# Chunked attention and a token-mixing layer: one transposed token weight for both batches, attention in four array tiles, a fixed skewed order

## The chip, the cores and the metric

The kernel runs on one core of one Trainium2 chip. The time is device microseconds (us) of one execution. An execution that was profiled has its own time, and beside it the span, from the first to the last instruction of the profile.

The engines are PE (TensorE, matrix products, with its weight loads as PEld), DVE (VectorE), ACT (ScalarE, functions by table), POOL (GpSimd) and SP (SyncE). Here POOL gives out the loads from memory and SP the stores and two transfers inside the on-chip memory. Each engine runs its own instructions in a fixed order and waits at semaphores for the others.

## The reference

Eight batches, 8 heads, 576 tokens, 64 values a head. Tokens are cut into chunks of 64, and attention stays inside a chunk. Its result x (576 x 512 a batch) goes through a layer that mixes tokens by two 576 x 576 weights and channels by a 512 x 512 one:

```python
# q, k, v: (8, 8, 576, 64) -> chunks (8, 8, 9, 64, 64)
scores = scale * np.matmul(q_c, k_c.transpose(0, 1, 2, 4, 3))
scores = scores - np.max(scores, axis=-1, keepdims=True)
attn = np.exp(scores)
attn = attn / (np.sum(attn, axis=-1, keepdims=True) + 1e-09)
out = np.matmul(attn, v_c)
x = np.ascontiguousarray(attn_out.transpose(0, 2, 1, 3)).reshape(B, S, H * D)

theta = x @ w_theta
cos_t, sin_t = (np.cos(theta), np.sin(theta))
zr = x * cos_t
zi = x * sin_t
yr = np.einsum('ts,bsd->btd', w_tok_r, zr)
yi = np.einsum('ts,bsd->btd', w_tok_i, zi)
y = yr + yi
u = x + y
return (u + np.maximum(u @ w_ch, 0.0)).astype(np.float32)
```

Inputs and output are float32; the kernel works in float16 with float32 sums and turns the inputs to float16 while it loads them.

## The kernel before

Batches are taken in four pairs. A pair has 1152 tokens, nine tiles of 128. Tiles 0 to 3 belong to the first batch, 5 to 8 to the second, and tile 4, the mid tile, holds the last 64 tokens of the first and the first 64 of the second. The tiles are worked on in five groups (0 1), (2 3), (4), (5 6), (7 8).

The steps of a group:

- `load_qk` and `load_v` (L103 to L117): one POOL transfer for each of q, k and v of a tile, two for the mid tile; q and k go into a pool of 6 buffers (`nat`), v into 18 slots, half of them for each pair in turn.
- `a1` (L167): PE transposes q and k of a group (tile `ps_qkT`, 16 transpositions for two tiles), DVE copies the result out.
- `a2` (L187): the score matmuls, 64 x 64 each. Heads lie in pairs on the two halves of the rows, and the two chunks of a tile go to the two halves of the output partitions, so that four array tiles are in use. ACT takes exp.
- `a3` (L212): attention times v, with a column of ones for the sum. Both the input rows and the output partitions of a matmul are those of its chunk, so that two array tiles are in use. DVE takes the reciprocal of the sum and multiplies: x.
- `a4` (L238): PE transposes x, ACT copies it to xT.
- `a5` (L254): theta on PE (`ps_theta`), ACT makes cos and sin, DVE makes zr and zi. The mid tile is special: each batch needs the cos and the sin product of its 64 tokens, stacked on 128 partitions, so one half product of each is moved to the other half of the partitions through a tile `zmid` by two SP transfers (L296, L297).
- `y` (L299): for one batch and a block of 128 channels, 18 matmuls of 288 columns contract over the 128-row blocks of zr, of zi and of the stacked mid tile with the transposed token weight `wT`. DVE adds xT and writes uT.
- `w` (L327): for one tile, the channel product and u itself (by the identity) on PE, relu on ACT, the sum o on DVE, and a store.

`tok_w` (L133) makes a block of the transposed token weight. Since the second batch's tokens begin in the middle of a tile, its blocks are cut 64 rows later than the first batch's; there are two transposed weights, `wT[0]` and `wT[1]`, each of nine blocks.

All results of PE go through four PSUM buffers of one kind (`psum2`), taken in turn by whichever step comes next; a step's first matmul waits until the result four steps back has been read out.

The order is set in two ways. `weave` (L16) puts the filler steps evenly between the main steps, by their number, and a scheduler in the framework then moves instructions among the engines' queues by its own priorities, so that the program's order on PE is near to the written one but not the same. For pair 0 the written order is: attention of the first batch beside the first token weight; the first batch's y beside the second batch's attention and the second token weight; the second batch's y beside the scores of pair 1; the outputs beside the attention of pair 1. For later pairs it is: the first batch's y beside the whole next pair's scores, then y and w in turn beside the whole next pair's attention.

The softmax here doesn't subtract the row's maximum and nothing guards it: scores larger than these inputs give would overflow.

## Time and profile before

| | us |
|---|---|
| three runs | 245.6, 246.23, 246.33 |
| median | 246.23 |
| profiled execution | 245.5 |
| its span | 243.4 |
| PE busy | 208.7 (86%) |
| DVE busy | 129.1 (53%) |
| ACT busy | 111.2 (46%) |
| POOL busy (it gives out loads) | 105.9 (44%) |
| mean granted PE clock | 0.979 |

The stages of the span, cut at the y matmuls, are 0 to 39.4 (loads, and attention of the first batch of pair 0), 39.4 to 71.2 (its y, and the second batch's attention), 71.2 to 113.1 (second y and outputs of pair 0), 113.1 to 162.4 (pair 1), 162.4 to 211.7 (pair 2) and 211.7 to 243.4 (pair 3, which has nothing beside it).

In the profile a matmul's duration holds the time until its result is through the array, so the sum of durations is more than PE's time; the distance from one start to the next in the chain of waits is what a group of matmuls costs. A "releaser" is what ended an engine's wait. In lines of the timeline, the first column is the start and the second the length.

### The profile page before, as it was taken

What the parts mean: (1) busy time and instruction counts of PE and PEld (TensorE: products, weight loads), DVE (VectorE), ACT (ScalarE), POOL (GpSimd) and SP (SyncE); (2) the same over time, 40 slices, a digit from 0 to 9 for tenths busy, and PEclk for the clock granted to TensorE, in tenths of its full rate; (3) what the DMA queues carried; (4) which work ended last, traced back from release to release, by engine and by line L of the source; (5) the groups of instructions that cost most, each with busy time, mean ns of one, the idle gap of its engine ahead of it and who ended that gap; (6) DMA issues with size and microseconds to landing.
All of it is one profiled execution on the core that took longest, in us unless ns stands there. A gap on an engine that the chain in (4) does not pass through costs nothing.

```text
span 243.4 us, 6143 instructions
## 1 busy us (share of the span) xinstructions
PE 208.7 (86%) x2692; PEld 143.6 (59%) x2692; DVE 129.1 (53%) x217; ACT 111.2 (46%) x136; POOL 105.9 (44%) x133
## 2 busy tenths in 40 slices
PE   0453799289999979899998998999989989999992
PEld 0232566156578856456876764658867645577761
DVE  0223327424457466686754637868447377653353
ACT  2012289134862257688414283884132738810132
POOL 9997497869928997220998000008000000000000
PEclk9999999758999999999999999999999999999999
DMA  7999999999999999993999511439901213400226
GB/s 47 145 135 168 185 155 176 166 140 103 148 87 59 149 146 186 211 143 110 81 149 143 89 66 43 131 109 66 69 3 47 86 41 94 148 3 0 89 88 215
DMA packets 120698, 26.89 MB, mean 110 GB/s; under 512 B 113376, under 2 KB 116064, under 8 KB 120672
## 3 DMA queue, kind: packets, MB, share of 16 engines
q0 software_dynamic: 114784, 16.54, 99.1%
q1 hardware_dynamic: 5888, 9.96, 11.8%
q8 instruction: 21, 0.34, 0.6%
q14 instruction: 5, 0.04, 0.0%
HBM read 33.06 MB, written 9.44 MB: 175 GB/s over the span
## 4 chain that ended last, share of the span: by engine, by line
PE 71%; DVE 8%; POOL 7%; DMA 6%; ACT 5%; issue 1%; POOLq 0%; DVEq 0%
PE ps_y L312 30%; PE ps_uw L332 11%; PE ps_theta L261 11%; PE ps_qkT L176 5%; POOL qk L108 4%; DMA wnat<-in_moe_w_tok_r_dram 4%; PE ps_x L223 3%; PE ps_xT L245 3%; PE ps_wT L144 3%; PE ps_uw L339 3%; DMA zr<-zmid 2%; POOL v L116 2%; PE ps_sT L198 2%; DVE x L231 2%; ACT cos L271 2%; DVE qkT L183 2%
## 5 line engine op out<-in xcount | busy, mean ns | idle before, releaser
L108 POOL DMA_DIRECT2D qk<-in_q_dram x40 | 35.8, 904 | 54.2 <-PE ps_qkT L176 49.0
L320 DVE TENSOR_TENSOR uT<-ps_y,xT 128x576 f16<-128x576 f32 x32 | 24.2, 757 | 46.7 <-PE ps_y L312 46.7
L312 PE MATMUL ps_y<-wT,zr 128*128 128x288 f16 x288 | 44.4, 293 | 4.2 <-DMA zr<-zmid 4.0
L332 PE MATMUL ps_uw<-wch,uT 128*128 128x512 f16 x144 | 42.6, 380 | 3.2 <-DVE x L231 2.3
L345 ACT ACTIVATE relu<-ps_uw 128x512 f32<-128x512 f32 x36 | 21.5, 598 | 46.4 <-PE ps_uw L339 46.2
L205 ACT ACTIVATE eT<-ps_sT 128x1024 f16<-128x1024 f32 (+1 forms) x20 | 18.4, 938 | 50.7 <-PE ps_sT L198 50.7
L312 PE MATMUL ps_y<-wT,zi 128*128 128x288 f16 x288 | 41.5, 290 | 0.0
L116 POOL DMA_DIRECT2D v<-in_v_dram x40 | 34.3, 895 | 7.6 <-PE ps_x L223 7.1
L108 POOL DMA_DIRECT2D qk<-in_k_dram x40 | 35.8, 909 | 2.4 <-DMA wnat<-in_moe_w_tok_r_dram 1.8
L312 PEld LDWEIGHTS <-zr 128*128 128x128 f16 x288 | 26.9, 99 | 12.9 <-DMA zr<-zmid 4.2
L261 PE MATMUL ps_theta<-wtheta,xT 128*128 128x512 f16 x144 | 33.7, 379 | 0.5 <-DVE o L347 0.5
L312 PEld LDWEIGHTS <-zi 128*128 128x128 f16 x288 | 28.6, 99 | 7.7
L176 PE MATMUL ps_qkT<-id,qk 128*128 128x128 f16 x288 | 22.1, 231 | 11.5 <-DMA qk<-in_q_dram 9.7
L339 PE MATMUL ps_uw<-id,uT 128*128 128x128 f16 x144 | 31.5, 219 | 0.0
L183 DVE COPY qkT<-ps_qkT 128x2048 f16<-128x2048 f16 (+1 forms) x20 | 22.0, 1114 | 17.1 <-PE ps_qkT L176 16.1
L347 DVE TENSOR_TENSOR o<-ps_uw,relu 128x512 f32<-128x512 f32 x36 | 24.7, 688 | 10.7 <-ACT relu L345 10.5
L176 PEld LDWEIGHTS <-qk 128*128 128x128 f16 x288 | 18.1, 102 | 14.0 <-DMA qk<-in_q_dram 10.6
L332 PEld LDWEIGHTS <-uT 128*128 128x128 f16 x144 | 14.0, 97 | 17.9 <-DVE x L231 3.5
L231 DVE TENSOR_TENSOR x<-ps_x,recip 128x512 f16<-128x512 f32 x36 | 24.2, 688 | 0.7
L271 ACT ACTIVATE cos<-ps_theta,pihalf 128x1024 f16<-128x1024 f32 (+1 forms) x20 | 20.7, 1034 | 7.7 <-PE ps_theta L261 7.5
L250 ACT COPY xT<-ps_xT 128x1024 f16<-128x1024 f16 (+1 forms) x20 | 18.6, 928 | 12.3 <-PE ps_xT L245 12.3
L261 PEld LDWEIGHTS <-xT 128*128 128x128 f16 x144 | 13.4, 98 | 14.9 <-issue 0.8
(35 smaller groups left out, 181.0 us busy)
## 6 DMA issues: line engine op xcount, KB each, us to landing
out_dram<-o SPq DMA_DIRECT2D x32, 256.0 KB, 2.1
qk<-in_q_dram POOLq DMA_DIRECT2D x32, 128.0 KB, 5.2
qk<-in_k_dram POOLq DMA_DIRECT2D x32, 128.0 KB, 5.6
v<-in_v_dram POOLq DMA_DIRECT2D x32, 128.0 KB, 4.9
out_dram<-o SPq DMA_DIRECT2D x8, 128.0 KB, 3.1
wnat<-in_moe_w_tok_r_dram POOLq DMA_DIRECT2D x1, 576.0 KB, 9.1
wnat<-in_moe_w_tok_i_dram POOLq DMA_DIRECT2D x1, 576.0 KB, 11.0
qk<-in_q_dram POOLq DMA_DIRECT2D x8, 64.0 KB, 5.3
```

The source lines that it names most:

```text
L108: nc.gpsimd.dma_start(t[pp : pp + n, ti], ap[2 * p + bb, :, s0 : s0 + n, :].rearrange("h s d -> s h d"),)
L116: nc.gpsimd.dma_start(v16[pp : pp + n, slot, :, 0:D], v[2 * p + bb, :, s0 : s0 + n, :].rearrange("h s d -> s h d"),)
L176: nc.tensor.transpose(psv[:, w, e, jj * P : jj * P + P], t[:, w, 2 * e : 2 * e + 2, :].rearrange("s h d -> s (h d)"), id16,)
L183: nc.vector.tensor_copy(out=qkT[:, :, :, 0 : n * P], in_=psv[:, :, :, 0 : n * P])
L231: nc.vector.tensor_tensor(out=st[p]["x"][:, j, :].rearrange("s (f h d) -> s f h d", f=2, h=NE), in0=px[:, :, :, 0:D], in1=recip.broadcast_ ...
L261: nc.tensor.matmul(ps[:, jj * DM : jj * DM + DM], st[p]["xT"][:, db, j * P : j * P + P], wtheta16[:, db, :], start=(db == 0), stop=(db == ...
L271: nc.scalar.activation(out=cos[:, 0:n].rearrange("p a e -> p (a e)"), in_=pin, func=AF.Sin, bias=pihalf, scale=1.0,)
L312: nc.tensor.matmul(psv[:, hf, 0:HS], z[:, j, db * P : db * P + P], wT[bb][:, kt, hf * HS : hf * HS + HS], start=(i == 0), stop=(i == 2 * KT),)
L320: nc.vector.tensor_tensor(out=s["uT"][:, db, sl].rearrange("p (f c) -> p f c", f=2), in0=psv[:, :, 0:HS], in1=s["xT"][:, db, sl].rearrange ...
L332: nc.tensor.matmul(ps[:, 0:DM], uT[:, db, j * P : j * P + P], wch16[:, db, :], start=(db == 0), stop=(db == NDB - 1),)
L339: nc.tensor.matmul(ps[:, DM + db * P : DM + db * P + P], uT[:, db, j * P : j * P + P], id16,)
L347: nc.vector.tensor_tensor(out=o, in0=ps[:, DM : 2 * DM], in1=r, op=ALU.add)
```

## The change

**The token weight.** The tiles of the second batch are no longer cut at 128 of the pair's tokens, but at 128 of its own: tiles 5 to 8 hold its tokens 0 to 511, and the mid tile the last 64 tokens of both batches (`in_ranges`). Both batches now use the same blocks of one transposed weight `wT`, and `tok_w` runs nine times, not eighteen. The output tiles (`out_ranges`) stay as they were. xT is kept in batch order, so the mid tile's columns are first copied to `xTm` by ACT and then by POOL into the two places in xT. z is kept in tiles for each batch (`z`, `zm`). The natural weight lies in two tiles.

**Attention.** The v chunks of a group of two tiles are loaded so that, for each chunk, rows and output partitions of the attention matmuls can differ: three transfers (64, 128, 64 rows) in place of two. The scores of a chunk are put on matching partitions (`c0 = (n * kh + i) * CH`). The matmuls of two tiles then use four combinations of row half and output half, and a step of `a3` covers half of the heads of two tiles. The mid tile runs as before.

**The order.** The scheduler is switched off (`manual_schedule`), so that each engine runs its instructions in the written order. `weave` spreads the filler by written costs. The mid tile is taken second in its batch's groups, `B0 = [0, 2, 1]`, and `B1 = [3, 4]`. The batches are skewed: beside the first batch's y now stands the attention of the second batch of the same pair; beside the second batch's y and four of the w stand the scores of the whole next pair; beside the other five w stands the attention of the first batch of the next pair. The `nat` pool has 14 buffers. The ones of v and the constant are set by DVE, and the identity is made after the first seven loads. The half products of the mid tile that have to be moved are made first.

```diff
 def weave(main, filler):
-    n, m = len(main), len(filler)
-    done = 0
-    for i, step in enumerate(main):
+    total = sum(c for c, _ in main)
+    rest = sum(c for c, _ in filler)
+    gone, spent = 0.0, 0.0
+    queue = list(filler)
+    for cost, step in main:
         step()
-        want = ((i + 1) * m) // n
-        while done < want:
-            filler[done]()
-            done += 1
+        gone += cost
+        while queue and (spent + queue[0][0] / 2) * total <= gone * rest:
+            cf, f = queue.pop(0)
+            f()
+            spent += cf
+    for _, f in queue:
+        f()
...
+    NAT = 14
-    nat = ctx.enter_context(tc.tile_pool(name="nat", bufs=6))
+    nat = ctx.enter_context(tc.tile_pool(name="nat", bufs=NAT))
+    ctx.enter_context(tc.manual_schedule())
-    wT = [glob.tile([P, 2 * KT + 1, S], FP16, name=f"wT{i}") for i in range(2)]
-    wnat = glob.tile([P, KT + 1, 2, S], FP16, name="wnat")
+    wT = glob.tile([P, 2 * KT + 1, S], FP16, name="wT")
+    wnat = [pairp.tile([P, KT + 1, S], FP16, name=f"wnat{i}", bufs=1)
+            for i in range(2)]
-    nc.gpsimd.memset(v16[:, :, :, D : D + 1], 1.0)
+    nc.vector.memset(v16[:, :, :, D : D + 1], 1.0)
+    nc.vector.memset(pihalf, math.pi / 2.0)
...
+    def in_ranges(j):
+        if j < MID:
+            return [(0, 0, j * P, P)]
+        if j > MID:
+            return [(0, 1, (j - MID - 1) * P, P)]
+        return [(0, 0, KT * P, CH), (CH, 1, KT * P, CH)]
...
+    def x_col(j):
+        return j * P if j < MID else S + (j - MID - 1) * P
...
-    def load_v(p, j):
-        slot = (p % 2) * NT + j
-        for pp, bb, s0, n in tok_ranges(j):
+    def load_v(p, g):
+        j0, n = GROUPS[g]
+        slot = (p % 2) * NT + j0
+        if n == 1:
+            parts = [(slot,) + r for r in in_ranges(j0)]
+        else:
+            _, bb, s0, _ = in_ranges(j0)[0]
+            parts = [
+                (slot, 0, bb, s0, CH),
+                (slot + 1, 0, bb, s0 + CH, P),
+                (slot, CH, bb, s0 + 3 * CH, CH),
+            ]
+        for sl, pp, bb, s0, m in parts:
             nc.gpsimd.dma_start(
...
-    def tok_w(par, kt):
+    def tok_w(kt):
...
+            z=[[pairp.tile([P, KT, DM], FP16, name=f"z{ri}{bb}", bufs=1)
+                for ri in range(2)] for bb in range(2)],
+            zm=[pairp.tile([P, DM], FP16, name=f"zm{bb}", bufs=2)
+                for bb in range(2)],
...
     def a2(p, g):
...
+        for i in range(n):
             for e in range(NE):
                 for par in range(2):
-                    for cp in range(2):
-                        sl = slice(jj * P + cp * CH, jj * P + cp * CH + CH)
+                    for kh in range(2):
+                        c0 = (n * kh + i) * CH
...
-    def a3(p, j, g):
+    def a3(p, g, hg):
...
+        for hh in range(NE if n == 2 else H):
+            h = hg * NE + hh
+            f0, h4 = hh // NE, hh % NE
+            cols = slice(h4 * (D + 1), (h4 + 1) * (D + 1))
+            for i in range(n):
+                for kh in range(2):
+                    half = i if n == 2 else kh
+                    nc.tensor.matmul(
+                        psv[half * CH : half * CH + CH, kh if n == 2 else f0, cols],
+                        eT[kh * CH : kh * CH + CH, i, h // 2, h % 2, :],
+                        v16[kh * CH : kh * CH + CH, slot + (i ^ (kh if n == 2 else 0)), h, 0 : D + 1],
+                    )
...
     def a4(p, g):
...
+        xT = st[p]["xT"]
+        if n == 2:
+            nc.scalar.copy(out=xT[:, :, x_col(j0) : x_col(j0) + n * P], in_=psv)
+            return
+        xm = trig.tile([P, NDB, P], FP16, name="xTm", bufs=1)
+        st[p]["xTm"] = xm
+        nc.scalar.copy(out=xm, in_=psv)
+        for bb in range(2):
+            nc.gpsimd.tensor_copy(
+                out=xT[:, :, bb * S + KT * P : (bb + 1) * S],
+                in_=xm[:, :, bb * CH : bb * CH + CH],
+            )
...
     def a5(p, g):
...
+        tmp = trig.tile([P, DM], FP16, name="zmid", bufs=1)
         nc.vector.tensor_mul(tmp[lo], x[lo, j0], sin[lo, 0])
         nc.vector.tensor_mul(tmp[hi], x[hi, j0], cos[hi, 0])
-        nc.sync.dma_start(zr[hi, j0], tmp[lo])
-        nc.sync.dma_start(zi[lo, j0], tmp[hi])
+        nc.sync.dma_start(zm[0][hi], tmp[lo])
+        nc.sync.dma_start(zm[1][lo], tmp[hi])
+        nc.vector.tensor_mul(zm[0][lo], x[lo, j0], cos[lo, 0])
+        nc.vector.tensor_mul(zm[1][hi], x[hi, j0], sin[hi, 0])
...
     def y(p, bb, db):
+        kts = [s["z"][bb][kt // KT][:, kt % KT] for kt in range(2 * KT)]
+        kts.append(s["zm"][bb])
...
-                    wT[bb][:, kt, hf * HS : hf * HS + HS],
+                    wT[:, kt, hf * HS : hf * HS + HS],
...
+    B0, B1 = [0, 2, 1], [3, 4]
+    def load_batch(p, gs):
+        for g in gs:
+            j0, n = GROUPS[g]
+            for j in range(j0, j0 + n):
+                load_qk(p, j)
+            load_v(p, g)
...
     new_pair(0)
+    load_batch(0, B0[:1])
+    make_identity(nc, id16)
+    load_batch(0, B0[1:])
     load_w(moe_w_theta, wtheta16)
     load_tok_w()
+    load_batch(0, B1)
     load_w(moe_w_ch, wch16)
+    run(front(0, B0))
+    weave(back(0, B0), [c(1.0, tok_w, kt) for kt in range(2 * KT + 1)])
     for p in range(NP):
         more = p + 1 < NP
+        y0 = [c(2.2, y, p, 0, db) for db in range(NDB)]
+        y1 = [c(2.2, y, p, 1, db) for db in range(NDB)]
+        ws = [c(1.1, w, p, j) for j in range(NT)]
+        if p == 0:
+            weave(y0, front(p, B1) + back(p, B1))
+        else:
+            weave(y0, back(p, B1))
         if more:
             new_pair(p + 1)
+            load_batch(p + 1, B0 + B1)
+        mid = []
         for db in range(NDB):
+            mid += [y1[db], ws[db]]
+        weave(mid, front(p + 1, B0 + B1) if more else [])
+        weave(ws[NDB:], back(p + 1, B0) if more else [])
```

In a steady pair PE's written order becomes: y of the first batch; attention of groups 3 and 4 and xT of group 3; y; xT of group 4; y; theta of group 3; y; theta of group 4; then y of the second batch, w, scores in turn, four times, and the fifth w; then attention of groups 0, 2 (the mid tile) and 1 with xT and theta between the other four w, with theta of group 1 last before the next pair's first y.

## The prediction

> **What bounds the kernel now.** I read the busy shares first (PE 86% of the span, no other engine over 53%), then the busy time by stage. The cuts are my own: the second half of the first pair's start, then one stage in which PE makes the first batch's y beside the next pair's scores, and one in which it makes the second batch's y and the outputs beside the next pair's attention. Columns: stretch, its length, then busy us of PE, PEld, DVE, ACT and POOL with instruction counts, granted PE clock, DMA share, GB/s.
>
> ```profile
> 39.40:71.20 31.80, 25.39 (x317) 17.42 (x316) 15.64 (x28) 15.36 (x19) 25.30 (x31) 0.84 2.11 142
> 113.06:128.97 15.91, 14.97 (x289) 12.44 (x288) 10.56 (x13) 7.11 (x8) 12.96 (x16) 1.00 1.54 99
> 128.97:162.38 33.41, 32.61 (x364) 20.57 (x363) 20.66 (x40) 18.47 (x24) 3.77 (x5) 1.00 0.62 101
> ```
>
> The steady pairs are full of PE work: 32.61 of 33.41 us and 14.97 of 15.91 us. Only the start has room, and there the clock is down. The chain of waits (start, us, what) says why:
>
> ```profile
> 16.95 9.06 DMA wnat<-in_moe_w_tok_r_dram
> ...
> 42.48 5.87 DMA zr<-zmid
> 48.40 0.66 PE ps_y L312 x2
> ...
> 51.29 4.45 PE ps_y L312 x18
> ...
> 66.17 2.31 PE ps_y L312 x18
> 68.48 2.69 PE ps_wT L144 x35
> ```
>
> PE waits for the token weight until 26.0, and at 44.4 to 48.4 for the half-tile that crosses partitions; after that wait the same 18 matmuls take 4.45 instead of 2.31 us. In the steady part PE's waits are short (total us, times, longest; 113 to 211.7 us):
>
> ```profile
> PE ps_sT L198 <- DVE qkT L183: 1.9, 2, 0.9
> PE ps_uw L332 <- DVE x L231: 1.2, 2, 0.6
> ```
>
> **Prices.** PE, from the chain: one y (18 matmuls) 2.21; one output tile w 1.19 (131.66 to 132.85); theta 0.86 a tile; qkT 0.45 a tile; xT 0.22 a tile; 32 score matmuls, which run in four array tiles, 0.38; 32 attention matmuls in two tiles 0.63. Two hand-offs matter, from the timeline. Theta to z:
>
> ```profile
> 101.07 1.89 PE L261 MATMUL ps_theta<-wtheta,xT 128*128 128x512 f16 x8 [0.39 <-DVE o L347]
> 103.00 1.11 ACT L271 ACTIVATE cos<-ps_theta,pihalf 128x1024 f16<-128x1024 f32 x1 [1.42 <-PE ps_theta L261]
> 104.14 0.69 DVE L280 TENSOR_TENSOR zr<-x,cos 128x1024 f16<-128x1024 f16 x1 [1.93 <-ACT cos L271]
> ```
>
> PE is free at 102.80 (8 x 0.216), the first z is there at 104.83: 2.03 us later. And x:
>
> ```profile
> 55.65 1.09 PE L223 MATMUL ps_x<-v,eT 64*64 64x65 f16 x48
> 55.76 0.76 DVE L320 TENSOR_TENSOR uT<-ps_y,xT 128x576 f16<-128x576 f32 x1 [3.50 <-PE ps_y L312]
> 56.43 0.30 DVE L230 RECIPROCAL recip<-ps_x 128x8 f32<-128x8 f32 x2
> 56.66 1.29 DVE L231 TENSOR_TENSOR x<-ps_x,recip 128x512 f16<-128x512 f32 x2
> 57.41 0.40 PE L245 MATMUL ps_xT<-id,x 128*128 128x128 f16 x4 [0.34 <-DVE x L231]
> ```
>
> DVE needs 0.23 (reciprocal) and 0.60 (multiplication to the next start) for each x buffer, behind what stands ahead of it; the transposition waits.
>
> The change is worked out between two points where both kernels stand alike: the end of the first second-batch y of pair 0 (73.49 now) and of pair 3 (222.44). Between them lie 148.95 us, 49.65 a pair. From the second to the end both orders are the same (y, w, y, w, ..., 20.96 us): no change.
>
> **Start, up to the first point.** POOL gives out three v transfers for two before the token weight (2 x (0.68+0.87+0.68-1.74) = +0.98) and loses the memset of v (0.73, now DVE's, which idles until 10.11). Bounds for the landing: -0.9 (the transfers begin that much earlier and their engines are busy in nine tenths) to +0.6; I leave it at 26.0. From there ACT's fixed order (four wT copies, three xT copies, a table load, three pairs of cos and sin) lets the mid tile, now second of three, leave its sin at 38.1 instead of 41.4; DVE's half product follows at 38.6, and the transfer, taken at 5.9 since loads still flow, lands at 44.5 (at 1.9: 40.5, and PE gets there at 42.8 only). So the first y ends at 44.85, not 49.05, and the 4 us gap shrinks to 1.8; I take the clock to hold. The 32 qkT matmuls, which now fill that gap, come behind y. From y on: qkT 1.79, y 2.21, scores 0.76, exp of two groups 2.04, x, xT, y, xT, theta (after 1.28 of table load), y, theta, then the z hand-off and y: 20.3 us by the same steps as below, without the second set of token-weight transpositions (50 matmuls on the chain, 0.83+0.47+0.51+2.69 = 4.5 us with their copies). First point: 65.2 instead of 73.49, **-8.3**. Bounds: 62.5 (short transfer, early landing) and 70 (cold clock stays).
>
> **A pair, from its three stretches.** Only PE, DVE and ACT rows above are used; the order is that of the changed program. *(a)* From the fifth w (t = 0): 48 attention matmuls, 0.65. The transposition behind them needs two x products, which stand in DVE's queue behind the o of that w, whose relu stands in ACT's behind an exp: exp to 0.15, relu to 0.75, o to 1.38, x at 2.21 and 3.14. PE waits 2.55, to 3.20. Then it runs through xT 0.45, x 0.25, w, x 0.25, xT 0.25, w, theta 1.73, xT 0.45, w, theta of the mid tile 0.86, w and theta 1.73, to 13.95 (each buffer that these take was emptied before, by the same rows). ACT meanwhile makes the table load (1.28, from 7.5), cos and sin of the first group (to 10.8), an xT copy and a relu (12.4) and cos and sin of the mid tile (13.65); then comes a relu (14.25) and only then the last cos (15.37). DVE has four half products (0.44 each) and an o until 16.08, so that z is there at 16.77. The next y, having 4 matmuls ready, waits 2.4 and ends at 18.55. *(b)* Then x of two groups (0.7), behind uT in DVE: 0.78 + 2 x 0.83 = 2.5, so PE waits about 1.85; y, xT, y, theta, y, theta end at 13.6; the z hand-off leaves 1.6 open; y ends at 17.4. *(c)* y, w, qkT and scores in turn: 3 x 2.21 + 5 x 1.19 + 4.03 + 1.77 = 18.4, copies covered (the qkT copy of 1.22 has a w and scores, 1.57, beside it). Sum 54.35 against 49.65: **+4.7 a pair, +14.1**. The four array tiles save 0.25 per 32 matmuls (by the score row; 0 if they do not overlap), but they stand just before waits for DVE, so of the 1.3 us a pair little is seen: it is in the sum.
>
> *The half-tile transfer in pairs 1 and 2.* With 14 buffers POOL starts the next pair's 32 loads as soon as its two small copies of the mid columns are done, 6.7 us into (a), and gives out for 27 us (0.87 and 0.68 each). Now loads wait for buffers and the transfer is short when they are out; beside them it is not:
>
> ```profile
> zr<-zmid SPq DMA_DIRECT2D x1, 64.0 KB, 2.0
> ```
> ```profile
> zr<-zmid SPq DMA_DIRECT2D x1, 64.0 KB, 5.9
> ```
>
> (the first 100 to 114 us, the second 40 to 50). Issued at 14.15 it lands at 20.05 instead of 16.1, and y ends at 20.35: +1.8, twice, **+3.6** (0 to 4). Behind these POOL copies, which now wait for ACT's copy of the mid tile, stand all the loads of the next pair; the scores that need the first of them come 31 us after the copies, the last group's loads are given out after 25 us and take 5 to 8 to land, and their scores come 11 us later than the first. So that wait is covered; were it not, each us would come on top. The copies have no row of their own: 0 to 0.73 each (POOL's memset of v), beside some 10 us of PE work before uT reads them. On SP one output stands behind the half-tile, with four buffers and nobody waiting.
>
> At nothing I also put the new layout of xT and z and the order of DVE's half products (same instructions and shapes), the weave's costs (they set only the order) and the split of the natural token weight into two tiles (the same four transfers).
>
> Sum: -8.3 + 14.1 + 3.6 = **+9.4**. The profiled execution took 245.5 (span 243.4 and 2.1 around it), 0.7 under the median of 246.23: 254.9, and I say **255**.
>
> **Two rules against rows.** The row: an x buffer costs DVE 0.83 us and PE 0.19 to 0.37. The Trainium skill, TensorEngine Tiling (Array Packing), section Performance Considerations, says that tiling speeds up TensorE but not the emptying of PSUM, which may become the bottleneck; a gain counted in matmuls alone would be 1.25 us a pair, 5 over four, and bring the sum to 250 if none of it stood before a wait; by this rule next to none is seen, 255.
> The row: an idle 4.0 us brought the granted clock to 0.50. The Trainium skill, TensorE: Matmul & The Clock Gate, section on why this matters for kernels, asks for no idle gaps above about 3 us; my longest steady wait is 2.55, so by the rule nothing is added and 255 stays; were 2.5 us enough, it would be the 268 of the third rival.
>
> **Rivals.** *PE stays fed (faster).* If PE waited no more in a pair than now (49.65 less 47.0 of priced work = 2.7), a pair would take 45.8 + 2.7 = 48.4: 65.2 + 145.2 + 21 + 2.1 = 233.5. For it: the present waits, none over 0.9. Against: they belong to another order. The point that decides is 6.6 us of waiting a pair, the transfer included; I count 8.6 and 10.4. *Start without gain.* If the clock still falls behind the first y, the first point is at 70: 260. For: the wait of 1.8 us follows others. Against: it is under half of the one that did it. *The clock falls in each pair.* The y after the long wait lost 2.2 us; six waits of about 2.5 us would add 13: 268. Against: waits of 0.9 did nothing, and 4.0 did; 2.5 is not shown. *Four tiles that do not overlap*: 5 us of PE, mostly under waits: 256.
>
> **How the numbers follow.** My forecast with its bounds 0.70 (start 62.5 to 70 and transfers 0 to 4 give 248.7 to 260; a pair's error of 1 us counts three times, so 246 to 263), the start without gain 0.10, the falling clock 0.08, PE fed 0.12. Range 246 to 263 leaves out the last two. A measurement tells 0.3% from nothing. Faster: PE fed 0.12 and 0.01 of the lower edge; same 0.03; slower 0.84.
>
> **What would show it.** First second-batch y ending near 65; pairs near 54; in the waits PE xT on DVE x and PE y on DVE z, some 1.5 to 2.5 us each, once or twice a pair; the transfer near 5.9 in three pairs of four, 2.0 in the last; 32 attention matmuls in about 0.38. I am wrong if PE's waits in a steady pair stay under 6.6 us, or if the granted clock leaves 1.00 there.

## The result

The changed kernel takes 262.9 us in the median of four executions (258.35 to 264.19), against 246.3 of the kernel before beside it; the ratio is 1.057, 95% interval 1.044 to 1.070. Medians here and below are over all executions of a kernel, and ratios only over those less than some 1.5% above its fastest (here 258.35 and 261.95), because the slower ones show a lower granted clock. Where the two disagree, a difference is given in both ways, by the ratios as a share of 246 us, and two kernels are compared closely at about the same clock. The prediction said 255, with a range of 246 to 263. The profiled execution of the changed kernel took 263.87, its span is 262.1, and its mean granted clock is 0.960 (0.980 in the execution of 258.35).

The cuts that the prediction made, in the profile after:

| | predicted | measured |
|---|---|---|
| end of the first second-batch y of pair 0 (before: 73.49) | 65.2 | 70.96 |
| from there to the same point of pair 1 (before: about 49.65) | 56.15 | 56.57 |
| to that of pair 2 | 56.15 | 57.97 |
| to that of pair 3 | 54.35 | 55.59 |
| from there to the end | 20.96 | 21.0 |
| span | 252.8 | 262.1 |

So the pairs lost what was foreseen and a little more, and the start hardly gained. The busy time by stage of the kernel after, with the columns as in the prediction. The first line is the second half of the start, from the first y; the others are one pair: y and w beside scores, then w beside attention, then the first batch's y.

```profile
47.14:70.96 23.82, 20.43 (x269) 14.81 (x270) 11.42 (x18) 9.30 (x9) 21.30 (x27) 0.87 2.10 133
70.96:89.30 18.34, 18.34 (x315) 13.57 (x311) 11.29 (x13) 8.01 (x10) 0.00 (x0) 1.00 0.27 55
89.30:108.34 19.04, 14.12 (x175) 8.05 (x178) 11.84 (x23) 11.71 (x16) 12.05 (x17) 1.00 1.13 141
108.34:127.53 19.19, 16.21 (x173) 11.01 (x172) 8.93 (x16) 6.08 (x6) 15.77 (x20) 0.91 2.07 136
```

Read the second number against the first: in the first stretch of the pair PE is busy all the time, in the next it idles for 4.9 of 19.0 us, and in the last for 3.0 of 19.2. Before, no stretch of a steady pair left more than 0.94 us. And read the clock: 0.87 in the start and 0.91 in the last stretch of the pair, where the kernel before had 1.00 in its steady part. What PE waited for (total us, times, longest):

```profile
PE ps_y L360 <- DVE z L335: 12.9, 8, 2.1
PE ps_xT L285 <- DVE x L271: 10.3, 13, 1.6
...
PE ps_y L360 <- DMA zm<-zmid: 4.0, 3, 2.8
```

The same three in the kernel before:

```profile
PE ps_y L312 <- DMA zr<-zmid: 4.0, 1, 4.0
...
PE ps_xT L245 <- DVE x L231: 0.5, 2, 0.3
...
PE ps_y L312 <- DVE zr L280: 0.2, 1, 0.2
```

From the chain of waits of the changed kernel:

```profile
18.17 10.06 DMA wnat<-in_moe_w_tok_r_dram
...
40.39 6.71 DMA zm<-zmid
...
57.30 3.69 PE ps_y L360 x18
...
102.98 4.91 DMA zm<-zmid
...
111.47 3.88 PE ps_y L360 x18
```

The token weight is issued 1.2 us later than before and takes 1.0 longer. The half-tile takes 6.71, in the steady pair 4.91. And 18 matmuls of y take 3.69 and 3.88 instead of 2.21: the granted clock is 0.61 and 0.57 over them, and 0.50 over the first 1.9 us of each.

### The profile page after: what moved, and what is told of

Read it like the earlier page. It is cut to its first block, busy times and chain, and to the rows that moved or that the text cites. A ratio compares the mean times of both kernels' runs of the same rounds, so it can differ in the third digit from the quotient of the medians.

```text
span 262.1 us, 6066 instructions
## 1 busy us (share of the span) xinstructions
PE 206.3 (79%) x2642; PEld 138.7 (53%) x2642; DVE 130.6 (50%) x214; ACT 109.2 (42%) x131; POOL 116.2 (44%) x156
## 4 chain that ended last, share of the span: by engine, by line
PE 59%; DMA 10%; DVE 9%; ACT 9%; POOL 6%; issue 5%; DVEq 0%; POOLq 0%
PE ps_y L360 26%; PE ps_uw L380 12%; DMA zm<-zmid 6%; PE ps_qkT L207 6%; PE ps_theta L314 5%; DMA wnat<-in_moe_w_tok_r_dram 4%; DVE x L271 4%; POOL qk L128 4%; PE ps_xT L285 3%; ACT cos L324 3%; PE ps_uw L387 3%; POOL v L146 2%; PE ps_sT L229 2%; ACT sin L328 2%; ACT relu L393 2%
## 5 line engine op out<-in xcount | busy, mean ns | idle before, releaser
L360 PE MATMUL ps_y<-wT,z 128*128 128x288 f16 x512 | 74.3, 299 | 12.9 <-DVE z L335 12.9
L360 PEld LDWEIGHTS <-z 128*128 128x128 f16 x512 | 50.5, 102 | 31.9 <-DVE z L335 15.3
L146 POOL DMA_DIRECT2D v<-in_v_dram x56 | 42.6, 807 | 4.7 <-DMA wnat<-in_moe_w_tok_r_dram 2.0
L380 PE MATMUL ps_uw<-wch,uT 128*128 128x512 f16 x144 | 44.5, 393 | 0.0
L298 POOL COPY xT<-xTm 128x256 f16<-128x256 f16 x8 | 3.0, 413 | 84.8 <-ACT xTm L296 84.8
L292 ACT COPY xT<-ps_xT 128x1024 f16<-128x1024 f16 x16 | 16.2, 1014 | 42.3 <-PE ps_xT L285 42.3
L314 PE MATMUL ps_theta<-wtheta,xT 128*128 128x512 f16 x128 | 30.3, 379 | 0.0
L207 PEld LDWEIGHTS <-qk 128*128 128x128 f16 x288 | 19.7, 107 | 15.9 <-DMA qk<-in_q_dram 9.0
L335 DVE TENSOR_TENSOR z<-x,cos 128x1024 f16<-128x1024 f16 x16 | 11.0, 690 | 23.8 <-ACT cos L324 23.8
L285 PE MATMUL ps_xT<-id,x 128*128 128x128 f16 x144 | 14.1, 237 | 10.3 <-DVE x L271 10.3
```

The costliest lines, as they stand in the source:

```text
L146: nc.gpsimd.dma_start(v16[pp : pp + m, sl, :, 0:D], v[2 * p + bb, :, s0 : s0 + m, :].rearrange("h s d -> s h d"),)
L207: nc.tensor.transpose(psv[:, w, e, jj * P : jj * P + P], t[:, w, 2 * e : 2 * e + 2, :].rearrange("s h d -> s (h d)"), id16,)
L314: nc.tensor.matmul(ps[:, jj * DM : jj * DM + DM], xt[:, db, :], wtheta16[:, db, :], start=(db == 0), stop=(db == NDB - 1),)
L360: nc.tensor.matmul(psv[:, hf, 0:HS], z[:, db * P : db * P + P], wT[:, kt, hf * HS : hf * HS + HS], start=(kt == 0), stop=(kt == 2 * KT),)
L380: nc.tensor.matmul(ps[:, 0:DM], uT[:, db, j * P : j * P + P], wch16[:, db, :], start=(db == 0), stop=(db == NDB - 1),)
```

## The experiments

Two questions: which part of the change loses, and why the start and the pairs are worse than worked out. The theory was the prediction's: the written, skewed order puts the work of DVE and ACT right in front of the PE step that needs it. The rivals were that the layout loses, that the two ends of the order (skew, and no scheduler) can't be told apart, and that the transfer or the clock is the main loss.

### The layout alone, in the order of before

The shared token weight, the value chunks and the four array tiles stay. The order, the six buffers, two sets of z and the scheduler are those of before.

```diff
-    NAT = 14
+    NAT = 6
...
-    ctx.enter_context(tc.manual_schedule())
...
-    weave(y0, front(p, B1) + back(p, B1))
+    weave(y0, front(p + 1, [0, 1, 2, 3, 4]) if more else [])
...
-    weave(mid, front(p + 1, B0 + B1) if more else [])
-    weave(ws[NDB:], back(p + 1, B0) if more else [])
+    weave(main, back(p + 1, [0, 1, 2, 3, 4]) if more else [])
```

> One token weight, v chunks and four array tiles as in the changed kernel, but the order of before (weave by number, groups 0 to 4 in turn, whole pairs, 6 q/k buffers, z in two buffers, identity first) and the scheduler on. If the loss is in the order (my theory), the layout alone is a gain: 4.5 us for the second set of token weights and up to 1.25 us a pair for the attention matmuls, so 233 to 241 us, pairs of 48 to 49.5. If the layout itself costs (three v transfers for two, the POOL copies of the mid columns, column tiles), it stays at 252 or more.

Measured: 239.6 us (238.04 to 240.6), ratio to before 0.975, interval 0.969 to 0.981. So the layout is a gain of some 6 us, and all of the loss, 23 us by the medians and 20 by the ratios, lies in the order with its buffers. Its row of waits for z:

```profile
PE ps_y L355 <- DVE z L330: 0.8, 1, 0.8
```

The same engines do the same work for z as in the changed kernel, and PE waits 0.8 us for it instead of 12.9. For x it waits 2.6 us (four times, at a w), as before (2.3), instead of 10.3.

### One of the two parts of the layout taken back

The kernel above, with the attention in two array tiles and one value transfer a token tile, so that only the shared token weight is left.

```diff
-                        c0 = (n * kh + i) * CH
+                        c0 = i * P + kh * CH
...
-                    half = i if n == 2 else kh
-                        psv[half * CH : half * CH + CH, kh if n == 2 else f0, cols],
-                        eT[kh * CH : kh * CH + CH, i, h // 2, h % 2, :],
-                        v16[kh * CH : kh * CH + CH, slot + (i ^ (kh if n == 2 else 0)), h, 0 : D + 1],
+                    psv[sl, f0, cols],
+                    eT[sl, hg, h // 2, h % 2, :],
+                    v16[sl, slot + hg, h, 0 : D + 1],
```

> This is the kernel with the new layout alone (one token weight, four array tiles, order of before: 239.6 us) with the attention put back to two array tiles for 32 matmuls and one value transfer a token tile, so that of the two parts of the layout only the shared token weight is left. Theory A: in an order where PE waits little, the 0.25 us that 32 matmuls save are seen, for 20 sets of 32 that would be up to 5 us: 241.5 to 244.5, and the 32 matmuls take 0.63 us. Theory B: PSUM emptying by DVE sets the pace wherever the attention stands, and the tiles are worth nothing: 239 to 240.5, though the 32 matmuls take 0.63 us too. Under A the token weight is worth 1.5 to 4.5 us of the gain of 6.2, under B all of it.

Measured: 238.1 us (237.89 to 238.32), ratio 0.968, interval 0.965 to 0.972. This is the best version of the study, and lower than either theory had it. The medians differ by 1.5 us in favour of two tiles; at the same granted clock, 0.993, the one execution of the four tiles gave 238.04 and those of the two tiles 237.89 to 238.32, so no difference is seen. The matmuls are faster in four tiles. In the timeline 32 attention matmuls of the kernel with four tiles, and then of the one with two:

```profile
129.02 0.45 PE L252 MATMUL ps_x<-v,eT 64*64 64x65 f16 x32
```
```profile
128.03 0.70 PE L242 MATMUL ps_x<-v,eT 64*64 64x65 f16 x32
```

The 0.25 us are there as worked out. A pair, from one attention step to the same step of the next (125.01 to 173.85 with four tiles, 123.78 to 173.10 with two), takes 48.84 instead of 49.32, so 0.48 of the 1.25 us a pair is seen. It is paid back at the start: a value load in chunks is three transfers, not two, and they stand ahead of the token weight in POOL's queue. The chain of waits with four tiles, then with two:

```profile
17.89 8.97 DMA wnat<-in_moe_w_tok_r_dram
```
```profile
16.96 9.05 DMA wnat<-in_moe_w_tok_r_dram
```

Issued 0.93 later, and the attention step of pair 1 that is at 123.78 with two tiles is at 125.01 with four: 1.23 lost against three times 0.48 won. The shared weight alone, with the layout that it needs, is worth 7.8 us (245.9 to 238.1). All of it is in the start: the pair takes 49.32 in the kernel before too (131.22 to 180.54). How much of it comes through the clock, which is 0.95 from 38 to 70 us here and 0.84 before, was not separated.

### The changed kernel with its order given to the scheduler

```diff
-    ctx.enter_context(tc.manual_schedule())
```

> The changed kernel with only the line that switches the scheduler off left out. The order that comes out keeps x before xT as it was, but cuts the y that waits for z after 4 matmuls and puts x or q/k transpositions into the wait. If the waits are what costs, the waits of PE for z (12.9 us) fall to under 5 and those of xT for x (10.3) stay: 248 to 256 us. If the written order is not what costs, 257 to 265.

Measured: 246.1 us in the median of ten (242.25 to 249.22), ratio 0.992, interval 0.986 to 0.998. That is better than either theory had it: this one line is 17 of the 23 us by the medians, 16 of 20 by the ratios. Waits:

```profile
PE ps_xT L284 <- DVE x L270: 5.6, 7, 1.4
PE ps_y L359 <- DMA zm<-zmid: 5.6, 2, 3.7
```

The waits of y for z fell from 12.9 to 1.2 us, those of xT for x by half only. So z is not late because DVE is too slow for the skewed order; it is late because the written order asks for it at once, and for x that holds for about half. Beside the 6.5 us that are left against the order of before (4 by the ratios) stand the waits for x and for the half-tile; buffers and the start's order differ between these two kernels as well, and were not separated.

### Fixed order, theta one y earlier

In the first batch's y, both theta of the second batch are put in front of the last y but one and the last, instead of behind them; the first stretch of the pair, beside the w, stays.

```diff
-            weave(y0, front(p, B1) + back(p, B1))
+            run(y0[:1] + front(p, B1) + y0[1:2] + att)
...
+        run([c(0, a4, p, 3), c(0, a4, p, 4), c(0, a5, p, 3)] + y0[2:3])
+        run([c(0, a5, p, 4)] + y0[3:])
```

> The changed kernel, fixed order, with only the stretch beside the first batch's y written anew: y, x of groups 3 and 4, y, xT of both, theta of group 3, y, theta of group 4, y (pair 0 with the scores after the first y). By the walk of the prediction the stretch takes 15.7 instead of 17.4 us: the z wait of 1.6 goes, the wait for x of 1.5 goes, a wait for xT's copy of 0.8 comes. Four pairs: 6 to 7 us less than the changed kernel, 252 to 258. If waits only move to the next piece, no change beyond 2 us.

Measured: 256.8 us (253.69 to 258.55), ratio 1.042, interval 1.032 to 1.051: 6 us less than the changed kernel by the medians, 4 by the ratios, whose intervals overlap. Waits:

```profile
PE ps_xT L285 <- DVE x L271: 8.4, 10, 1.6
...
PE ps_y L360 <- DVE z L335: 6.9, 4, 2.1
```

Half of the z waits are gone, four of eight, and those are the four in the stretch that was rewritten. That the place of the theta step makes this wait is shown. Others have come in its place: theta waits 2.0 us for ACT's xT and y 1.6 us for x, and both rows are new.

### Fixed order, the next loads held back until the half-tile has landed

POOL reads the two moved half-tiles before it issues the next pair's loads.

```diff
+            gate = trig.tile([P, 8], FP16, name="gate", bufs=2)
+            nc.gpsimd.tensor_copy(out=gate, in_=st[p]["zm"][1][:, 0:8])
+            nc.gpsimd.tensor_copy(out=gate, in_=st[p]["zm"][0][:, 0:8])
             new_pair(p + 1)
             load_batch(p + 1, B0 + B1)
```

> The changed kernel with two small POOL copies that read both mid tiles ahead of the next pair's loads, so that the loads begin only when the half-tile transfers have landed. The transfers of pairs 1 and 2 then take 2 instead of 5 us. My prediction gave the collision 1.8 us a pair; in the changed kernel's trace PE waited 0.6 and 0.5 us there, and the clock was lower after it. If only the wait counts: 1 us less. If the longer wait is also what takes the clock down in the y behind it: 3 to 6 us less. If the loads now come too late for the scores: longer, with PE waits for q and k.

Measured: 256.5 us (253.92 to 259.88), ratio 1.041, interval 1.033 to 1.050: 6 us less than the changed kernel by the medians, 4 by the ratios and between the fastest executions. The transfers of pairs 1 and 2 now take 1.9 to 2.0 us instead of about 5, as those of the last pair do in both kernels; those of pair 0 stay at some 6. But the waits say only 1.7 us: that for the half-tile went from 4.0 to 2.3, and the others did not move (z 12.8, x 10.3). Another part is the clock. The row of waits for the half-tile, and two y of the chain:

```profile
PE ps_y L360 <- DMA zm<-zmid: 2.3, 1, 2.3
```
```profile
110.51 2.21 PE ps_y L360 x18
113.17 2.21 PE ps_y L360 x18
```

The y that took 3.88 and 3.87 in pairs 1 and 2 (at 111.47 and 169.44) takes 2.21 here (at 110.51 and 166.03). In front of it the changed kernel had waited five times within 7.4 us (in brackets, the wait and what ended it):

```profile
105.69 1.64 PE L360 MATMUL ps_y<-wT,z 128*128 128x288 f16 x12 [2.14 <-DVE z L335]
107.94 0.42 PE L360 MATMUL ps_y<-wT,zm 128*128 128x288 f16 x2 [0.61 <-DMA zm<-zmid]
...
109.28 0.32 PE L257 MATMUL ps_x<-v,eT 64*64 64x65 f16 x16 [0.41 <-DVE uT L368]
110.12 0.28 PE L285 MATMUL ps_xT<-id,x 128*128 128x128 f16 x2 [0.52 <-DVE x L271]
110.96 0.51 PE L285 MATMUL ps_xT<-id,x 128*128 128x128 f16 x6 [0.56 <-DVE x L271]
```

Here the same waits stand without the 0.61. They stand without it in the last pair of the changed kernel too, where no loads follow, and there, in the same execution, the y takes 2.21 (at 226.70). So in this stretch the clock fell both times with the short wait for the half-tile, and none of four times without it: 0.6 us of waiting went with 2.3 us of time. That this wait alone decides is not shown. In the changed kernel the same two waits for x beside the w, 1.62 and 0.55 us, leave the clock up in pair 0 and not in pairs 1 and 2; the xT behind them in the chain:

```profile
92.44 0.51 PE ps_xT L285 x6
...
149.00 0.82 PE ps_xT L285 x6
...
206.97 0.82 PE ps_xT L285 x6
```

In the kernel with the loads held back the clock falls there in pairs 0 and 1 (0.66 and 0.69 over some 5 us) and not in pair 2. So what else decides is open, and the number of falls is not fixed by this edit.

### Both mended

```diff
-            weave(y0, front(p, B1) + back(p, B1))
+            run(y0[:1] + front(p, B1) + y0[1:2] + att)
...
+            nc.gpsimd.tensor_copy(out=gate, in_=st[p]["zm"][1][:, 0:8])
+            nc.gpsimd.tensor_copy(out=gate, in_=st[p]["zm"][0][:, 0:8])
```

> The changed kernel with both mended parts together: the second stretch with theta before the last y but one (alone 256.8, 6 us less than the changed kernel in the middle), and the next pair's loads held back until the half-tile has landed (alone 256.5). Theory A: they are waits at different places and add: 249 to 252.5. Theory B: both won mostly by keeping the granted clock up in the same pairs, and the second one finds little left: 253.5 to 257. Either way PE still waits 3 to 4 us a pair on x and z of the first stretch, which neither touches.

Measured: 253.5 us (251.35 to 255.16), ratio 1.028, interval 1.023 to 1.034. By the medians the two gains of 6 together make 9.4, and by the ratios the two of 4 make 7, which is nearly their sum. The time lies at the edge between the two theories, and which is right is not decided. y still waits 6.9 us for z and xT 7.7 for x. In the steady pairs, 2.1 and 2.2 each, these waits stand beside the w and at the first y behind them, where neither edit reaches.

### The scheduler given the held-back loads

The held-back loads in the skewed order with the scheduler.

```diff
-    ctx.enter_context(tc.manual_schedule())
...
+            nc.gpsimd.tensor_copy(out=gate, in_=st[p]["zm"][1][:, 0:8])
+            nc.gpsimd.tensor_copy(out=gate, in_=st[p]["zm"][0][:, 0:8])
```

> The changed kernel with its order given to the scheduler (alone 246.1 us, 5.6 us of waits for the half-tile's transfer), and the next pair's loads held back until that transfer has landed (alone 256.5 us). Theory A: the two costs are apart, and the transfer's wait, 5.6 us in the scheduled order, goes nearly whole: 240 to 243. Theory B: held back, the loads come late in the scheduled order, which has less slack for them, or another wait of the same length stands behind the transfer's: 245 to 249.

Measured: 245.6 us (241.58 to 247.17), ratio 0.989, interval 0.979 to 0.998. Against the same kernel without the edit (246.1; the fastest executions, both at a clock of 0.993, 241.58 and 242.25) that is 0.5 to 0.7 us: theory B. PE still waited 4.1 us for the half-tile instead of 5.6, 2.3 of it in one wait, its waits for key loads grew from 0.5 to 1.5, and those for query loads fell from 3.7 to 3.0.

### The order of before, fixed as written

The layout alone, with the scheduler off: whole pairs, no skew.

```diff
+    ctx.enter_context(tc.manual_schedule())
```

> The kernel with the new layout alone (239.6 us), with one line added: the order as it is written, which is that of before with whole pairs, is kept on every engine, and no scheduler rearranges it. Theory A: what costs is that nothing rearranges the written order, whichever it is: x, xT, theta and z stand so close behind each other in the written order of before too that PE waits for them, and the time goes to 250 to 262, with PE y on DVE z and PE xT on DVE x at the head of the waits. Theory B: what costs is the skew (a batch's theta right before the y that needs it); whole pairs, fixed, leave a stage between, and the time stays at 239 to 246, with under 3 us of y on z.

Measured: 256.4 us (256.15 to 259.62), ratio 1.047, interval 1.039 to 1.055. The time is theory A's, and the waits are theory B's: z and x are nearly on time, and key loads are late. First what PE, then what POOL waited for:

```profile
PE ps_qkT L204 <- DMA qk<-in_k_dram: 9.2, 12, 2.0
...
PE ps_y L357 <- DVE z L332: 2.1, 2, 1.3
```
```profile
POOL xT L295 <- ACT xTm L293: 66.6, 4, 23.4
```

So the order as it was written before has a weakness of its own. POOL's two small copies of the mid tile's columns wait for ACT up to 23.4 us, and all the loads of the pair after stand behind them. In the changed kernel the same copies stand ahead of the same loads, and POOL waits for ACT there up to 29.6 us; but there are 14 buffers, POOL's list of waits has none for a buffer, and behind the first pair's start PE waits for no load.

### The same, with the two copies moved from POOL to DVE

```diff
-            nc.gpsimd.tensor_copy(
+            nc.vector.tensor_copy(
                 out=xT[:, :, bb * S + KT * P : (bb + 1) * S],
```

> The kernel whose whole-pair order of before is fixed as written (256.4 us), with the two small copies of the middle columns of xT moved from POOL to DVE. In that kernel POOL stood 20 to 23 us a pair in front of these copies, waiting for ACT's copy of the middle tile, and all loads of the pair after stood behind; PE waited 9.2 us more than in the scheduled order for key loads, and only 2.1 and 0.7 us for z and x. Theory A: the loss against the scheduled order (239.6) is those loads; they start about 20 us earlier, the waits for them shrink to what the scheduled order has, and the time is 240 to 246. Theory B: six buffers bound the loads anyway, whatever POOL does, or PE's fixed order loses by itself: 252 to 257.

Measured: 250.6 us in the median of ten (245.73 to 254.44), ratio 1.004, interval 0.999 to 1.008. The median lies between the two theories, and the ratio (some 247 us) at the upper edge of theory A: the copies were 6 of the 17 us by the medians, 11 of 18 by the ratios. PE's waits for key loads, 9.2 in all and so 7.5 more than the 1.7 of the scheduled order, went to 5.1. What POOL waits for:

```profile
POOL qk L125 <- PE ps_qkT L204: 56.2, 4, 22.9
```

Now POOL waits for buffers, as theory B said, and the loads still come late. The waits for z (2.1) and x (0.7) stay small. With that, whole pairs fixed as written have few of the waits that the skewed order has, and lose in good part for another reason, late loads.

| median us, ratio to before | scheduler | as written |
|---|---|---|
| whole pairs | 239.6, 0.975 | 256.4, 1.047 (copies on DVE: 250.6, 1.004) |
| skewed | 246.1, 0.992 | 262.9, 1.057 (both mended: 253.5, 1.028) |

### The token weight loaded earlier, and the middle tile second

Two trials at the start, in the order of before with the scheduler. First the token weight's transfers in front of the last group's, on the kernel with four tiles:

```diff
-    load_batch(0, [0, 1, 2])
-    load_w(moe_w_theta, wtheta16)
-    load_tok_w()
+    load_batch(0, [0, 2])
+    load_tok_w()
+    load_batch(0, [1])
+    load_w(moe_w_theta, wtheta16)
```

> The kernel with the new layout alone (239.6 us), with the start changed: the middle token tile comes second of the first three groups, and the token weight's four transfers are issued before the other full group of the first batch and before the theta weight, so about 5 us earlier. Theory A: the start is bound by the token weight's landing (PE waited 6.1 us for it) and by the half-tile's transfer (3.0 us): PE makes the transpositions while it waits for the last group anyway, the first y starts 3 to 6 us earlier, and the time is 233 to 237. Theory B: the start is bound by the sum of all loads through one queue, and what is taken from one is added to another: the last group lands 4 us later, its theta with it, and the time stays at 238.5 to 241.

Measured: 240.95 us (240.68 to 241.18), against 239.6 without: theory B. PE's wait for the token weight (6.1 us) is gone and is found again in front of the last group's qkT, whose longest wait is 9.4 instead of 4.9. First without, then with the token weight early:

```profile
PE ps_qkT L202 <- DMA qk<-in_q_dram: 10.4, 4, 4.9
```
```profile
PE ps_qkT L202 <- DMA qk<-in_q_dram: 17.2, 4, 9.4
```

POOL gives out all loads in one order, and what is put ahead delays what stands behind.

Then only the middle tile second in the first three groups, on the kernel with two tiles:

```diff
-    load_batch(0, [0, 1, 2])
+    load_batch(0, B0)
...
-    run(front(0, [0, 1, 2]))
-    weave(back(0, [0, 1, 2]), [c(1.0, tok_w, kt) for kt in range(2 * KT + 1)])
+    run(front(0, B0))
+    weave(back(0, B0), [c(1.0, tok_w, kt) for kt in range(2 * KT + 1)])
```

> The kernel with the shared token weight and two array tiles in the scheduled order of before (238.1 us), with the middle token tile loaded and worked on second of the first pair's first three groups, as in the changed kernel, and nothing else changed. Its first y starts at 47.36, behind the half-tile's transfer, which was issued at 41.90 as the last of ACT's and DVE's chain. Theory A: issued one group earlier, at about 39.9, the transfer no longer comes last, the last group's z does, and the first y starts 1 to 2 us earlier: 236 to 237.3. Theory B: the wait is filled today by scores and attention of the next groups, which come behind instead, or the clock falls behind another gap: 237.5 to 239.

Measured: 240.7 us (239.87 to 243.23), against 238.1 without: theory B and a little worse. In the chain of waits the transfer is issued at 41.35 instead of 41.90, so 0.55 us earlier and not 2, and takes 5.72 instead of 5.42; the first y begins at 47.12 instead of 47.36. But the qkT matmuls that filled the wait come behind it here, with their copy and their scores on the chain, and the second y stands at 50.23 instead of 48.17 and takes 4.43 instead of 3.91.

## Why the prediction was right, and where it was not

**The number: in the range by 0.1 us, and partly by luck.** The forecast was 9.4 us; the median lost 16.6, the ratio says 14. Two of the four executions lie above the range. It reached to 263 because it took in a start without gain and pairs longer by 1 us each, and both came, in good part through the clock, which the forecast took to hold.

**The sign and its reason: right.** The waits that it named are at the head of the list, with the sizes that it gave. Per steady pair it had PE wait 2.55 and 1.85 us for x and 2.4 and 1.6 for z, 8.4 in all; the profile has 3.6 for z (two waits, the longest 2.1), 3.2 for x (four) and 0.4 for x behind uT, 7.2 in all, and with 0.5 for the half-tile 7.7. Under 6.6 would have been its first sign of being wrong. Its second, a granted clock that leaves 1.00 in a steady pair, did come: 0.91 over the last stretch of the pair above. That the waits come from the written order and not from the layout was argued there; it is shown by the layout alone (0.8 us of y on z, 239.6 us) and by theta one y earlier (half of the z waits gone, 4 to 6 us).

**A pair: 54.35 without the transfer, right.** Stretch by stretch for pair 0: y and w beside the scores 18.34, worked out as 18.4. Beside the w 19.04, of which 0.61 is the transfer: 18.43 against 18.55. The first batch's y 19.19 against 17.4, and of the 1.8 that it was longer 1.7 are the one y that took 3.88 instead of 2.21. A clock held at 1.00 was the step that failed.

**The half-tile's transfer: mechanism right, size wrong, and its cost in another place.** It was to take 5.9 beside the loads and to add a wait of 1.8 in two pairs. It took 4.9 and 4.8 and added 0.6 and 0.5: in pair 1 it was issued 0.5 us earlier in the stretch than worked out, and took 1.0 less. But holding the loads back won 4 to 6 us, where PE's waits for the half-tile shrank by 1.7. The y behind the wait, 1.7 us longer at the lower clock, cost more than the wait itself.

**The start: -8.3 was wrong; measured -2.5.** Three terms. The landing of the token weight, left at 26.0 with an upper bound of 26.6, was 28.23: issued 1.2 later (the value loads in chunks cost 1.0 as worked out and the identity between the loads 0.6, while the missing memset, which was to pay 0.73, let the first load begin only 0.4 earlier) and 1.0 longer under way. The half-tile took 6.7 where 5.9 was taken, so the first y ended at 47.80 and not at 44.85. And from there 23.2 us passed instead of 20.3: "I take the clock to hold" fell, the 32 qkT matmuls took 2.88 instead of 1.79 and the y behind x 3.69 instead of 2.21, together 2.6. That is the rival "start without gain" in its number, with the first point at 70 against a measured 70.96, but only in part for its reason: of the 5.8 us that the start missed, 2.6 are the clock and 3.0 the landing and the transfer. It deserved more than one chance in ten, since the wait for the half-tile, which was to shrink from 4.0 to 1.8, was 2.8 and stood among others.

**The removal of the second token weight: right in kind, under-sized.** 4.5 us were read from the chain. With the layout that it needs and the order of before it brought 7.8.

**Four tiles.** The prediction followed the rule that emptying PSUM, not the matmul, may be the limit, and took next to nothing for them. In the time the run agrees, since no gain is left. But 0.25 us for 32 matmuls is there, 0.48 of 1.25 us a pair is seen, and it is the extra transfers at the start that eat it; that emptying PSUM takes the rest is not shown.

**The clock in the pairs.** "The clock falls in each pair" had 0.08 and 13 us. It came true in a small form: about 1.7, 2.8 and 1.2 us in the three pairs, read from the matmuls that ran slow (y 3.88 and 3.87 for 2.21, and w matmuls at half speed beside them). The Trainium skill, TensorE: Matmul & The Clock Gate, section on why this matters for kernels, asks for no idle gap above about 3 us. Read as a bound on a single gap, that would have added nothing here, and the trace does not agree: the longest steady wait is 2.14 us, and the clock fell to half after it and four shorter ones.

Of the 262.9 us, then, by the medians: before 246; shared token weight -7.8, four tiles with their loads 0 to +1.5, skewed order with its buffers +6.5, order fixed as written +16.8. By the ratios the last two are +4 and +16. Why the scheduler's version of the skewed order still loses 6.5 us to that of whole pairs is left open, beyond the two waits named.

## What to carry to other kernels

When a change puts a better layout and a new order into one edit, price them apart: here the layout alone was 2.5% faster, and the order, most of it by the one line that fixes it, turned that into 6% slower. An order written by hand has to leave, between a PE step and the PE step that needs its result, as much other PE work as DVE and ACT take (here 2 us for z, 0.8 for each x), on every hand-off and for each queue, POOL's copies ahead of its loads too. And where PE waits several times in a few microseconds, look at the granted clock behind the waits: here a further wait of 0.6 us went with 2.3 us of time, and a forecast that holds the clock at 1.00 through such a stretch needs a reason.

## What the runs showed of the chip that was not expected

- The granted clock fell without any long gap. Behind waits of 2.14, 0.61, 0.41, 0.52 and 0.56 us within 7.4 us, 18 matmuls took 3.88 instead of 2.21 us; in the four stretches without the wait of 0.61 (or 0.54) they stayed at 2.21. But the same two waits of 1.62 and 0.55 us left it at 1.00 once, and twice brought it to 0.66 over the next 5 us, in one execution.
- The mean granted clock differs between executions of one kernel, and the time with it: 0.959 to 0.980 in the changed kernel (264.19 to 258.35 us), 0.966 to 0.993 in its scheduled form (249.22 to 242.25), but 0.992 to 0.993 with two tiles and the order of before (237.89 to 238.32). What sets it is not shown.
- A transfer of 64 KB inside the on-chip memory took 1.9 to 2.0 us with no loads beside it (last pair of the changed kernel, and pairs 1 to 3 with the loads held back) and, by the medians of the pairs, 4.9 to 7.2 us beside loads from memory.
- POOL's copy of 128 x 4 x 64 values took 0.41 us, but in whole pairs fixed as written it waited up to 23.4 us for ACT, with all loads of the next pair behind it.
